# Slot-softmax denominators: from a ones product on TensorE and Ln/Exp on ScalarE to block transposes and a reduction on VectorE, in a fused attention and maxout-FFN kernel, with a new order of issue

## The chip, the cores and the metric

The kernel runs on one core of one Trainium2 chip. The metric is device time in microseconds (us), the median over several executions. The profile is of one execution; its "span" runs from the first to the last instruction that the profiler saw, and the measured time of the same execution is a little longer.

## The reference

Eight batches (b), eight heads (h), 576 positions (s), head size 64 (d), 32 memory slots (m). All inputs and outputs are float32.

```python
a = exp(phi - max_s(phi)); a = a / sum_s(a)              # softmax over positions
k_m = einsum('bhsm,bhsd->bhmd', a, k)                    # 32 slot keys per head
v_m = einsum('bhsm,bhsd->bhmd', a, v)                    # 32 slot values per head
p = exp(q @ k_m.T / 8 - max); p = p / sum_m(p)           # softmax over the 32 slots
x = (p @ v_m) as [4608 tokens, 512]
h = max(x @ w1, x @ w2, x @ w3)                          # maxout, 768 wide
out = h @ w_out                                          # [4608, 512]
```

The change concerns `sum_m(p)`, the denominator of the softmax over slots, and how batch 0 and the weights are brought in.

## The kernel before

Everything is computed in bfloat16 with float32 accumulation. Because `max(x@w1, x@w2, x@w3) = x@w3 + max(x@(w1-w3), x@(w2-w3), 0)`, the kernel multiplies with weight differences, and the part `x@w3` goes straight to the output through the product `w3 @ w_out`. And because `x = p @ v_m`, the slot values are multiplied into the weights first ("folded"), so that the FFN's first layer reads the 32 slot probabilities per head and not `x`.

The work of a batch is a set of small steps. Each is a letter, a number and `@batch` in one long string near the end of the kernel, and the program is issued in exactly that order: every engine receives its instructions in the order in which the steps stand there, and waits on semaphores where data or buffers are not ready. Nothing is reordered by a planner. An exclamation mark swaps the engine (ScalarE or VectorE) that empties a PSUM tile. The steps:

- `Y0 Y1 Y2 Y3` load w1, w2, w3 (L106, issued at L108) and w_out (L115). `L0 L1 L2 L3` load phi, k, v, q of a batch (phi at L90, k and v at L94, q at L102); `H` loads half of k or v for batch 0. All of these go through the POOL queue and convert to bfloat16 on the way, except phi, which stays float32; phi of batch 0 goes through SP (L88).
- `Zn` issues n warm-up matmuls (L132). `I` makes the identity matrix.
- `W0..W2` transpose w3 on TensorE (L157), emptied at L149; `O0..O3` compute w3 @ w_out (L165).
- `V` replaces w1 and w2 in place by w1 - w3 and w2 - w3 on VectorE (L186).
- `E` is exp(phi) on ScalarE (L203). `B` is k_m and v_m on TensorE (L216), `N` divides by the softmax denominators over positions (L232 to L246), `K` transposes the result into `kvt` (L261), emptied by ScalarE or VectorE.
- `Q` transposes half of a batch's q in 32x32 blocks on VectorE (L273).
- `S` makes the scores (L295) and their exponentials `e2` on ScalarE (L304), in two groups g = 0, 1 of four heads. `M` multiplies `e2` by a block matrix of ones, `blkones`, which leaves in each slot's row the sum over the 32 slots (L316). `R` turns the sum into its reciprocal on ScalarE by Ln and Exp(-x) (L329, L335). `X` multiplies on VectorE and gives `attn` (L340). `M`, `R` and `X` come once for each group.
- `D0..D2` (and `D4` for batch 0) fold the slot values into the weight differences, `D3` into w3 @ w_out (L361). Eight matmuls of 64x32 tiles stand side by side in each.
- `F0..F11` is the first FFN layer (L387), four matmuls each. An even one is emptied with Relu, mostly by ScalarE (L143); an odd one by VectorE, which takes the maximum with the even one (L400) into `hT`.
- `T0..T4` is the second layer: six matmuls with w_out (L418) and two or four with the folded w3 @ w_out (L427, L436), emptied into `ot` (L145 or L149) and stored through SP (L448).

All PSUM tiles come from one pool of four buffers of two banks each (tag `acc`), taken in turn in the order of issue; the `sm` tiles of step `M` are among them. k and v have one buffer for even and one for odd batches, q and phi two each.

Batch 0 before, up to the first step of the FFN:

```
H3@0 H2@0 H1@0 H0@0 L3@0 E@0 Z48@0 B@0 Y2@0 N@0 Y3@0 Q0@0 Q1@0 I@0 Z4@0 K@0! Z8@0 S@0
Z6@0 M1@0 R1@0 Y0@0 Y1@0 L0@1 M0@0 R0@0 W2@0 W1@0 W0@0 Z9@0 O0@0 X0@0 O1@0 X1@0 O2@0
O3@0 L1@1 V1@0 V0@0 D1@0 D0@0! L3@1 D3@0 V2@0 F8@0
```

Of the kernel before, what the change touches and what calls it, by code (L numbers as in the profile page):

```python
# [8 lines left out]
FP32 = mybir.dt.float32  # L9
# [6 lines left out]
def kernel(  # L16
# [12 lines left out]
    nc = tc.nc  # L29
# [145 lines left out]

    FIRST = {0: (0, 512), 1: (512, 768), 2: (768, 1024), 4: (1024, 1536)}

# [3 lines left out]
    def w_diff(n):  # L181

        c, end = FIRST[n]
        while c < end:
            e = min(end, (c // DF + 1) * DF)
            nc.vector.tensor_tensor(  # L186
                out=w12[:, :, c:e],
                in0=w12[:, :, c:e],
                in1=w_sb[:, :, 2, c % DF : c % DF + e - c],
                op=ALU.subtract,  # L190
            )
            c = e

# [58 lines left out]
    def att_kv_t(b, swap, part=None):  # L255

        s = st[b]
        ns = {None: slice(0, 3), 0: slice(1, 3), 1: slice(0, 1)}[part]
        ps = acc_pool.tile([P, 3, P], BF16, name="kvtp", tag="acc")
        for n in range(3)[ns]:  # L260
            nc.tensor.transpose(ps[:, n], s["kvn"][:, n], ident)  # L261
        if part != 1:
            s["kvt"] = work.tile([P, 3, P], BF16, name="kvt")
        evacuate("K", 0, swap, s["kvt"][:, ns], ps[:, ns])

    def att_q(b, n):
# [13 lines left out]
    def att_score(b):  # L280
# [3 lines left out]
        e2 = s["e2"] = work.tile([P, NG, S], BF16, name="e2")  # L284
        if b % 2 == 0:
            attns[b // 2] = work.tile([P, NG, 2 * S], BF16, name="attn")
# [23 lines left out]

    def att_sum(b, g):
        s = st[b]
# [11 lines left out]

    def att_rec(b, g):
        s = st[b]
# [10 lines left out]

    def att_mul(b, g):
        s = st[b]
        nc.vector.tensor_tensor(  # L340
            out=attns[b // 2][:, g, (b % 2) * S : (b % 2 + 1) * S],
            in0=s["e2"][:, g, 0:S],
            in1=s["r", g],
            op=ALU.mult,
        )

    wps, wp3s = {}, {}

    def fold(b, n, swap):
# [7 lines left out]
        ps = acc_pool.tile([P, NG, BANK], FP32, name="wps", tag="acc")  # L357
        for j in range(NP):
            for a in range(NG):
                r = slice(HP * a, HP * (a + 1))  # L360
                nc.tensor.matmul(  # L361
                    ps[M * j : M * (j + 1), a, 0 : hi - lo],
                    lhsT=s["kvt"][r, 0, M * j : M * (j + 1)],
                    rhs=(w3o if n == 3 else w12)[r, j, lo:hi],
                    start=True,
                    stop=True,
                    tile_position=(HP * a, M * j),
                )
        evacuate(
# [112 lines left out]
    def issue(b, n, swap):  # L482
# [12 lines left out]
            "S": lambda: att_score(b),  # L495
            "M": lambda: att_sum(b, i),
            "R": lambda: att_rec(b, i),
            "X": lambda: att_mul(b, i),
            "D": lambda: fold(b, i, swap),
# [9 lines left out]
    for w in """  # L509
        H3@0 H2@0 H1@0 H0@0 L3@0 E@0 Z48@0 B@0 Y2@0 N@0 Y3@0 Q0@0 Q1@0 I@0 Z4@0 K@0! Z8@0 S@0  # L510
        Z6@0 M1@0 R1@0 Y0@0 Y1@0 L0@1 M0@0 R0@0 W2@0 W1@0 W0@0 Z9@0 O0@0 X0@0 O1@0 X1@0 O2@0
        O3@0 L1@1 V1@0 V0@0 D1@0 D0@0! L3@1 D3@0 V2@0 F8@0 F10@0 F4@0 V4@0 F2@0 D2@0! F6@0!
        D4@0 F0@0 F3@0 F1@0 E@1 F5@0 F7@0 L2@1 F9@0 F11@0 B0@1 N0@1 T3@0 Q0@1 L1@2 L0@2 K0@1!
        T1@0 Q1@1 S@1 B1@1 N1@1 M0@1 L2@2 R0@1 K1@1 M1@1 X0@1 T0@0 R1@1 D1@1! L3@2 D0@1 D2@1
        E@2 X1@1 T2@0 F6@1! F10@1 F8@1 F7@1 F11@1 F0@1 F1@1 D3@1 B@2 F4@1 N@2 F9@1 L1@3 F5@1
        K@2! F2@1 Q1@2 F3@1 D3@2 L0@3 D2@2 T4@1! Q0@2 S@2 T0@1 M1@2 E@3 R1@2 M0@2 R0@2 T1@1!
        D0@2 L2@3 X1@2 D1@2! B@3 T2@1! L3@3 X0@2 L1@4 N@3 L0@4 F2@2 F6@2 Q1@3 Q0@3 F4@2 K@3
        F10@2 F0@2 F3@2 S@3 L2@4 F1@2 F8@2 L3@4 F11@2 M1@3 F7@2 R1@3 D3@3 E@4 D0@3! F9@2 T3@1
        F5@2 M0@3 R0@3 B@4 D2@3 D1@3! X1@3 N@4 L0@5 X0@3 T0@2! F0@3 F2@3 Q1@4 F4@3 Q0@4 L2@5
        F10@3 K@4 F6@3 F11@3 E@5 F3@3 D1@4! D0@4 T2@2! S@4 L1@5 F7@3 F8@3 F1@3 M0@4 F5@3 F9@3  # L520
        R0@4 X0@4 M1@4 R1@4 B@5 N@5 X1@4 D2@4 L3@5 D3@4 Q0@5 T2@3! K@5 F6@4 L3@6 F0@4 Q1@5 F4@4
        F7@4 S@5 F5@4 L0@7 F2@4 Q1@6 L0@6 Q0@6 F8@4 M1@5 R1@5 F1@4 E@7 F9@4 T1@2 F3@4 M0@5 R0@5
        L1@6 E@6 F10@4 T1@3 T3@3 X1@5 X0@5 F11@4 D3@5 D0@5 L2@6 B@6 D1@5! T0@3! N@6 L1@7 F2@5
        L2@7 F4@5 K@6 T4@3! S@6 B@7 D2@5 N@7 F3@5 F8@5 L3@7 F0@5 Q0@7 M0@6 R0@6 F1@5 T0@4! M1@6
        Q1@7 K@7 R1@6 T3@2 X0@6 X1@6 S@7 F5@5 F10@5 F6@5 F9@5 M1@7 R1@7 F7@5 X1@7 F11@5 M0@7
        R0@7 T3@4 X0@7 D2@7! D2@6 D0@7 T4@5! D1@6 D0@6 D1@7! T0@5! F0@7 F8@6 F4@6 F0@6 F6@6
        F9@6 F1@7 F10@6 F5@6 F11@6 F2@7 F6@7 F7@6 F2@6 F1@6 D3@6 D3@7 T1@4 F4@7 F3@6 F5@7 F3@7
        F8@7 F10@7 F11@7 F9@7 F7@7 T3@6 T1@5 T2@5! T2@7! T1@6 T0@7! T1@7 T2@6! T0@6! T2@4! T3@5
        T4@7! T3@7
    """.split():  # L530
# [32 lines left out]
```

## Time and profile before

| quantity | value |
|---|---|
| median of 8 runs | 171.08 us (170.21 to 171.70) |
| profiled execution: time | 171.5 us |
| profiled execution: span | 169.7 us |
| busy: TensorE matmuls / weight loads | 162.7 us / 91.3 us |
| busy: VectorE / ScalarE / GpSimd | 86.3 us / 112.6 us / 28.3 us |
| HBM read / written | 39.32 MB / 9.44 MB |
| first FFN matmul (F8@0) starts at | 30.38 us |

The profile gives, for each group of instructions, its line, engine, operation, operands (out<-in), shape, count, busy time in us, mean duration in ns, and how long the engine was idle before these instructions and what released it. PE is TensorE's matmul, PEld its weight load, DVE is VectorE, ACT ScalarE, POOL GpSimd, SP the sync engine. A busy engine is not yet the one that sets the time: the chain of waits, followed back from the last instruction, tells that. The profiled execution is 0.4 us above the median, and 1.8 us of its time lie around the span.

### The profile page before, as it was taken

The numbers are of one execution on the slowest core, as the hardware profiler recorded it, in microseconds if no ns is written. First come the engines' busy times: TensorE is split into PE (matmuls) and PEld (weight loads), VectorE is DVE, ScalarE is ACT, GpSimd is POOL, SyncE is SP. The second block draws the span as 40 slices with busy tenths as digits, with TensorE's granted clock in tenths as the row PEclk, the third lists the DMA queues.
The fourth block names the chain that finished last, engine by engine and source line by source line (L and its number), as shares of the span: only waits on it lengthen the run. The fifth ranks groups of instructions, "written<-read, shape, count | busy, mean of one in ns | idle before, by whom it ended". The sixth has DMA issues, their size and how long they took to land.

```text
span 169.7 us, 4672 instructions
## 1 busy us (share of the span) xinstructions
PE 162.7 (96%) x2015; PEld 91.3 (54%) x2035; DVE 86.3 (51%) x146; ACT 112.6 (66%) x170; POOL 28.3 (17%) x43
## 2 busy tenths in 40 slices
PE   7999999999799999999999999999999999999991
PEld 2344554574357446756566655564736757444450
DVE  6403174986368729588469773155862738100000
ACT  4100444863897898999999998797989682242420
POOL 7951111103302323100533100000000000000000
PEclk9999999999999999999999999999999999999999
DMA  5999999999999999999999999921113001243533
GB/s 155 174 204 210 203 211 265 222 207 261 259 227 307 233 217 325 258 278 229 239 237 349 234 208 234 256 98 62 62 68 124 0 4 62 85 162 128 184 124 126
DMA packets 21973, 31.77 MB, mean 187 GB/s; under 512 B 1216, under 2 KB 16576, under 8 KB 21952
## 3 DMA queue, kind: packets, MB, share of 16 engines
q0 software_dynamic: 16080, 21.43, 65.7%
q1 hardware_dynamic: 5728, 9.90, 16.5%
q8 instruction: 16, 0.26, 0.6%
q10 hardware_dynamic: 144, 0.13, 0.2%
q14 instruction: 5, 0.04, 0.1%
HBM read 39.32 MB, written 9.44 MB: 287 GB/s over the span
## 4 chain that ended last, share of the span: by engine, by line
PE 95%; issue 1%; DVE 1%; ACT 0%; ACTq 0%
PE acc L387 29%; PE po L418 27%; PE po L132 11%; PE po L427 8%; PE wps L361 5%; PE kvp L216 4%; PE po L165 3%; PE sm L316 2%; PE sc L295 2%; PE po L436 1%; PE kvtp L261 1%; PE po L459 1%; PE pt L157 1%; DVE kvn L236 0%; DVE kvn L246 0%
## 5 line engine op out<-in xcount | busy, mean ns | idle before, releaser
L387 PE MATMUL acc<-attn,wp 128*128 128x288 bf16 x384 | 52.2, 286 | 0.0
L418 PE MATMUL po<-wo_sb,hT 128*128 128x512 bf16 x194 | 50.3, 380 | 0.9
L400 DVE TENSOR_TENSOR hT<-acc,h 128x576 bf16<-128x576 f32 x48 | 34.8, 752 | 20.4 <-PE acc L387 19.2
L387 PEld LDWEIGHTS <-wp 128*128 128x128 bf16 x384 | 36.4, 98 | 13.1 <-issue 1.6
L145 ACT COPY ot<-po 128x512 f32<-128x512 f32 x31 | 18.2, 588 | 24.1 <-PE po L427 18.2
L418 PEld LDWEIGHTS <-hT 128*128 128x128 bf16 x210 | 19.5, 98 | 23.8 <-issue 3.5
L143 ACT ACTIVATE h<-acc 128x576 bf16<-128x576 f32 x46 | 27.5, 657 | 3.6 <-PE acc L387 3.6
L145 ACT CAST wp<-wps 128x1024 bf16<-128x1024 f32 x27 | 26.1, 1016 | 1.7 <-PE wps L361 1.7
L132 PE MATMUL po<-warm 128*128 128x512 bf16 x73 | 19.4, 423 | 1.4 <-DVE warm L120 1.2
L427 PE MATMUL po<-wp,attn 128*128 128x512 bf16 x61 | 18.2, 379 | 0.0
L132 PEld LDWEIGHTS <-warm 128*128 128x128 bf16 x75 | 7.7, 107 | 11.2 <-issue 3.8
L340 DVE TENSOR_TENSOR attn<-e,r 128x576 bf16<-128x576 bf16 x16 | 11.8, 753 | 2.7 <-PE po L427 1.4
L273 DVE STREAM_TRANSPOSE qT<-qq 128x576 f32<-128x576 f32 x16 | 11.7, 757 | 0.0
L329 ACT ACTIVATE ln<-sm 128x576 f32<-128x576 f32 x16 | 10.4, 647 | 1.5 <-PE sm L316 1.1
L335 ACT ACTIVATE r<-ln 128x576 f32<-128x576 f32 x16 | 10.9, 683 | 0.5
L304 ACT ACTIVATE e<-sc 128x576 bf16<-128x576 f32 x16 | 9.6, 662 | 2.2 <-PE sc L295 2.2
L476 DVE COPY ot<-po 128x256 f32<-128x256 f32 x1 | 0.4, 425 | 20.5 <-PE po L467 20.5
L203 ACT ACTIVATE e<-ph 128x1152 bf16<-128x1152 f32 (+1 forms) x9 | 9.5, 1060 | 1.6 <-DMA ph<-in_phi_dram 1.5
L94 POOL DMA_DIRECT2D kvo<-in_k_dram x9 | 6.7, 742 | 23.2 <-PE kvp L216 15.5
L427 PEld LDWEIGHTS <-attn 128*128 128x128 bf16 x62 | 6.1, 98 | 7.2
L102 POOL DMA_DIRECT2D qq<-in_q_dram x8 | 6.0, 748 | 22.2 <-DVE qT L273 18.0
L145 ACT COPY kvt<-kvtp 128x384 bf16<-128x384 bf16 (+1 forms) x3 | 1.3, 445 | 12.2 <-PE kvtp L261 12.2
(48 smaller groups left out, 118.4 us busy)
## 6 DMA issues: line engine op xcount, KB each, us to landing
out_dram<-ot SPq DMA_DIRECT2D x35, 256.0 KB, 2.4
qq<-in_q_dram POOLq DMA_DIRECT2D x8, 576.0 KB, 17.9
ph<-in_phi_dram POOLq DMA_DIRECT2D x7, 576.0 KB, 15.1
kvo<-in_k_dram POOLq DMA_DIRECT2D x7, 576.0 KB, 17.2
kvo<-in_v_dram POOLq DMA_DIRECT2D x7, 576.0 KB, 16.7
w_sb<-in_moe_w_dram POOLq DMA_DIRECT2D x3, 768.0 KB, 18.9
wo_sb<-in_moe_w_out_dram POOLq DMA_DIRECT2D x1, 768.0 KB, 16.5
ph<-in_phi_dram SPq DMA_DIRECT2D x2, 288.0 KB, 2.9
```

Of the source, the lines that this page charges most:

```text
L132: nc.tensor.matmul(po[:, 0:BANK], lhsT=warm[:, 0:P], rhs=warm, start=True, stop=True)
L143: nc.scalar.activation(out=out_, in_=in_, func=AF.Relu)
L145: nc.scalar.copy(out=out_, in_=in_)
L273: nc.vector.transpose(out=s["qT"][:, j].rearrange("p j c r e -> p (j c r e)").bitcast(FP32), in_=loaded[b]["q"][:, j].rearrange("p j c d - ...
L304: nc.scalar.activation(out=e2[:, a].rearrange("p (t r c) -> p t r c", t=2, c=NC), in_=sc[a][:, :, 0:SH].rearrange("p t (c r) -> p t r c", ...
L329: nc.scalar.activation(out=ln.rearrange("p (h n) -> p h n", h=2), in_=sm[:, :, 0:SH], func=AF.Ln,)
L335: nc.scalar.activation(out=r, in_=ln, func=AF.Exp, scale=-1.0)
L340: nc.vector.tensor_tensor(out=attns[b // 2][:, g, (b % 2) * S : (b % 2 + 1) * S], in0=s["e2"][:, g, 0:S], in1=s["r", g], op=ALU.mult,)
L387: nc.tensor.matmul(acc[:, h, 0:SH], lhsT=wps[b][:, g, w * DF + ft * P : w * DF + (ft + 1) * P], rhs=attn[:, g, c0 : c0 + SH], start=(g == ...
L400: nc.vector.tensor_tensor(out=hT[:, ft, (b % 2) * S : (b % 2 + 1) * S].rearrange("p (h n) -> p h n", h=2), in0=a, in1=s["h1", ft], op=ALU.max,
L418: nc.tensor.matmul(po, lhsT=hT[:, fc, c0 : c0 + P], rhs=wo_sb[:, fc, :], start=(n == 0), stop=False,)
L427: nc.tensor.matmul(po, lhsT=attn[:, g, c0 : c0 + P], rhs=wp3s[b][:, g, :], start=False, stop=(g == NG - 1),)
```

## The change

For batches 1 to 7 the steps `M` and `R` are replaced by steps on VectorE. `e2` is read as float32 words (two neighbouring bfloat16 positions each) and transposed in 32x32 blocks (`a`), so that the 32 slots of a head lie along the free dimension; they are summed there (`s`), the sums are inverted (`c`), the exponentials are multiplied by them (`m`), and the result is transposed back into `attn` (`X`). Batch 0 keeps the ones product, under new names. For batch 0 the folds into w1 and w2 no longer read weight differences: each is a sum of two products, one with w1 or w2 and the slot values, one with w3 and the negated slot values `kvtn`. The in-place subtraction `V` comes after the folds of batch 0, for batches 1 to 7. k and v of batch 0 are computed apart (`B0`, `B1`, and so on). The order is new throughout; at the start w3 and w_out are the first loads of the POOL queue, and the warm-ups become 29, then 9, 2 and 5.

```diff
-    FIRST = {0: (0, 512), 1: (512, 768), 2: (768, 1024), 4: (1024, 1536)}
+    FIRST = {0: (0, 384), 1: (384, 768), 2: (768, 1152), 4: (1152, 1536)}
...
-        c, end = FIRST[n]
+        c, end = n * BANK, (n + 1) * BANK
...
         evacuate("K", 0, swap, s["kvt"][:, ns], ps[:, ns])
+        if b == 0 and part != 0:
+            s["kvtn"] = const.tile([P, P], BF16, name="kvtn")
+            nc.scalar.mul(out=s["kvtn"], in_=ps[:, 0], mul=-1.0)
...
-    def att_sum(b, g):
+    def ones_sum(b, g):
...
-    def att_rec(b, g):
+    def ones_rec(b, g):
...
-    def att_mul(b, g):
+    def ones_mul(b, g):
...
+    def att_t(b, g):
+        s = st[b]
+        t = s["t", g] = work.tile([P, S // HP, R, 2], BF16, name="t", tag=f"t{g}")
+        nc.vector.transpose(
+            out=t.rearrange("p n r e -> p (n r e)").bitcast(FP32),
+            in_=s["e2"][:, g].bitcast(FP32),
+        )
+
+    def att_sum(b, g):
+        s = st[b]
+        sm = s["sm", g] = work.tile([P, S // HP, 2], FP32, name="sm", tag=f"sm{g}")
+        nc.vector.tensor_reduce(
+            out=sm,
+            in_=s["t", g].rearrange("p n r e -> p n e r"),
+            op=ALU.add,
+            axis=mybir.AxisListType.X,
+        )
+
+    def att_rec(b, g):
+        s = st[b]
+        nc.vector.reciprocal(out=s["sm", g], in_=s["sm", g])
+
+    def att_mul(b, g):
+        s = st[b]
+        t = s["t", g]
+        nc.vector.tensor_tensor(
+            out=t,
+            in0=t,
+            in1=s["sm", g].unsqueeze(2).to_broadcast([P, S // HP, R, 2]),
+            op=ALU.mult,
+        )
+
+    def att_back(b, g):
+        nc.vector.transpose(
+            out=attns[b // 2][:, g, (b % 2) * S : (b % 2 + 1) * S].bitcast(FP32),
+            in_=st[b]["t", g].rearrange("p n r e -> p (n r e)").bitcast(FP32),
+        )
...
-        for j in range(NP):
-            for a in range(NG):
-                r = slice(HP * a, HP * (a + 1))
-                nc.tensor.matmul(
-                    ps[M * j : M * (j + 1), a, 0 : hi - lo],
-                    lhsT=s["kvt"][r, 0, M * j : M * (j + 1)],
-                    rhs=(w3o if n == 3 else w12)[r, j, lo:hi],
-                    start=True,
-                    stop=True,
-                    tile_position=(HP * a, M * j),
-                )
+        terms = [(s["kvt"][:, 0], w3o[:, :, lo:hi] if n == 3 else w12[:, :, lo:hi])]
+        if b == 0 and n != 3:
+            terms.append((s["kvtn"], w_sb[:, :, 2, lo % DF : lo % DF + hi - lo]))
+        for i, (lhs, rhs) in enumerate(terms):
+            for j in range(NP):
+                for a in range(NG):
+                    r = slice(HP * a, HP * (a + 1))
+                    nc.tensor.matmul(
+                        ps[M * j : M * (j + 1), a, 0 : hi - lo],
+                        lhsT=lhs[r, M * j : M * (j + 1)],
+                        rhs=rhs[r, j, :],
+                        start=(i == 0),
+                        stop=(i == len(terms) - 1),
+                        tile_position=(HP * a, M * j),
+                    )
...
-            "M": lambda: att_sum(b, i),
-            "R": lambda: att_rec(b, i),
-            "X": lambda: att_mul(b, i),
+            "a": lambda: att_t(b, i),
+            "s": lambda: att_sum(b, i),
+            "c": lambda: att_rec(b, i),
+            "m": lambda: att_mul(b, i),
+            "X": lambda: (ones_mul if b == 0 else att_back)(b, i),
+            "M": lambda: ones_sum(b, i),
+            "R": lambda: ones_rec(b, i),
```

The new order up to the scores of batch 2:

```
Y2@0 I@0 Z29@0 W1@0 W0@0 Y3@0 W2@0 H2@0 H0@0 Z9@0 O3@0! E@0 L3@0 O0@0 B0@0 N0@0 O2@0
K0@0! Q0@0 H3@0 H1@0 O1@0 Q1@0 Y0@0 S@0 Z2@0 M0@0 R0@0 B1@0 Y1@0 N1@0 M1@0 R1@0 L0@1
K1@0 L1@1 D3@0 X0@0 Z5@0 D1@0! X1@0 D0@0 F10@0 F8@0 F0@0 F4@0 V0@0 F2@0! D2@0 D4@0 V1@0
F6@0 F1@0 F5@0 F11@0 F7@0 L3@1 F3@0 F9@0 E@1 B0@1 L2@1 N0@1 L0@2 Q0@1 T2@0! Q1@1 K0@1!
T1@0 S@1 V2@0 B1@1 L1@2 E@2 a0@1 s0@1 a1@1 N1@1 s1@1 T3@0 K1@1 c1@1 D0@1 D1@1! c0@1
m0@1 L2@2 D2@1 L3@2 m1@1 X0@1 T0@0! X1@1 F10@1 F4@1 L0@3 F11@1 F8@1 F0@1 F5@1 F2@1 F1@1
F9@1 F6@1 F7@1 F3@1 B@2 D3@1 T3@1 N@2 Q1@2 Q0@2 K@2 E@3 T4@1! L1@3 L2@3 S@2
```

## The prediction

> **What bounds the kernel now.** I read the chain of waits first, then the busy times, then the timeline of the first 31 us.
>
> ```profile
> PE 95%; issue 1%; DVE 1%; ACT 0%; ACTq 0%
> PE acc L387 29%; PE po L418 27%; PE po L132 11%; PE po L427 8%; PE wps L361 5%; PE kvp L216 4%; PE po L165 3%; PE sm L316 2%; PE sc L295 2%; PE po L436 1%; PE kvtp L261 1%; PE po L459 1%; PE pt L157 1%; DVE kvn L236 0%; DVE kvn L246 0%
> ```
>
> TensorE's own work is 95% of the chain; 11% of it are warm-ups (L132), which do nothing but pass time while data come. So there are two stages. From the first FFN matmul on, a table of engine busy times for that stretch alone gives:
>
> ```profile
> 30.38:166.08 135.70, 133.89 (x1761) 78.04 (x1777) 73.45 (x124) 103.00 (x155) 15.65 (x21) 1.00 0.79 185
> ```
>
> (window, sum; then busy us of PE, PEld, DVE, ACT, POOL.) TensorE is idle 1.8 of 135.7 us: here only less TensorE work, or an earlier start, shortens the kernel. Before 30.38 us the timeline shows what the first FFN matmul waited for:
>
> ```profile
> 23.98 5.34 PE L165 MATMUL po<-wo_sb,w3T 128*128 128x512 bf16 x23
> 26.05 1.83 DVE L186 TENSOR_TENSOR w_sb<-w_sb 128x1024 bf16<-128x1024 bf16 x2 [1.36 <-DMA w_sb<-in_moe_w_dram]
> 29.25 0.52 PE L361 MATMUL wps<-w_sb,kvt 64*32 64x256 bf16 x16
> 30.38 2.29 PE L387 MATMUL acc<-attn,wp 128*128 128x288 bf16 x16
> ```
>
> w1 landed at 26.0 us, but the folds L361 began at 29.25, because TensorE was busy until then with w3 @ w_out (L165), which could not begin before w_out had landed (issue at 5.67 us plus 16.5 to landing: 22.2), and whose first product also stood behind nine warm-ups.
>
> **The rows that the change touches.**
>
> ```profile
> L340 DVE TENSOR_TENSOR attn<-e,r 128x576 bf16<-128x576 bf16 x16 | 11.8, 753 | 2.7 <-PE po L427 1.4
> L273 DVE STREAM_TRANSPOSE qT<-qq 128x576 f32<-128x576 f32 x16 | 11.7, 757 | 0.0
> L329 ACT ACTIVATE ln<-sm 128x576 f32<-128x576 f32 x16 | 10.4, 647 | 1.5 <-PE sm L316 1.1
> L335 ACT ACTIVATE r<-ln 128x576 f32<-128x576 f32 x16 | 10.9, 683 | 0.5
> ```
>
> **What the Trainium skill says.** "VectorE: DVE Perf Modes", section on the TRN2 errata, gives (N+151)/0.96 GHz for an fp32 two-input operation: 757 ns at N = 576, and the two DVE rows above show 753 and 757. I use it as an estimate for the half-width transposes: (288+151)/0.96 = 457 ns. The same page's perf-mode tier table says `tensor_reduce` has only the 1x mode; at 576 elements that makes 757 ns by the same formula, an estimate, since no reduction is in this trace. "TensorE: Matmul & The Clock Gate", section "Wait — 56ns, not 53.3ns?", gives N/2.4 GHz + 2.5 ns from one warm matmul to the next, 122.5 ns at N = 288; the trace agrees, four `sm` matmuls take 0.49 us in the chain (61.21 us). The same page's Part 1 says that the clock starts at half rate until some 3.4 us of work; here warm-ups came 0.43 us apart until 6.67 us and 0.21 after.
>
> **The sum, part by part.**
>
> 1. *Ones products gone.* Seven batches x two groups x two matmuls = 28 matmuls x 0.1225 = **-3.4 us** on TensorE, all on the path. Batch 0 keeps its four. Their 14 PSUM tiles go too.
>
> 2. *Start.* The POOL loads before the FFN are the same bytes in another order. In the before trace the queue is steady: halves of k and v land 1.4 us apart (8.5, 9.9, 11.3), q 2.8 later (14.1), each weight 3.8 to 4.4 later (17.8, 22.2, 26.0, 29.9). So in the new order w3 lands at about 9.5, w_out 13.7, k 16.5, q 19.3, v 22.2, and w1 and w2 at 26.0 and 29.9 as before. The warm-ups Z29 end near 13x0.43+16x0.215 after 1.2 us, 10.2; W, Z9 and two of the O steps fill to 16.6; B0 is there when k is; O2, O1 fill up to q. Q0 and Q1 (2 x 0.757 after 19.3) give S@0 at 20.8 to 21.3. Then ScalarE is the chain: two exponentials (0.66 each), two Ln/Exp pairs (1.33 each), `kvtn` (0.3, estimated from the 0.38 of a 256-wide copy), D3's evacuation (1.02), D1's (768 elements between rows of 657 ns at 576 and 1016 at 1024: 0.80): 21.4 + 6.1 = 27.5. The other requirement, w1 at 26.0 + D1's matmuls 0.4 + 0.8, comes to 27.2. So F10@0 starts near 27.6, **-2.8 us**. The O steps (5.2 us) and the subtraction (1.8 us) leave the path because w_out comes 8 us earlier and the folds no longer need differences.
>
> 3. *Double folds of batch 0.* D1 and D0 lie in part 2. D2 and D4 become 32 matmuls of 384 columns instead of 16. By the 24 of 512 columns that take 0.77 us in the chain, that is 0.77 us against about 0.57: **+0.2 us**.
>
> 4. *VectorE chain.* Per group 0.457 + 0.757 + 0.18 (row of 167 ns for two columns, now 18) + 0.753 + 0.457 = 2.60 us instead of 0.753. `V` now stands among batch 0's FFN steps: V0 (1.22, row of 1219 ns) and V1 (two pieces of 0.69, row of 686 ns) are queued ahead of F2's Relu and of all `hT`, which T2@0 waits for; before, V2 and V4 stood there with 1.83 us, so I take nothing for the difference of 0.8, inside the bounds below. Splitting batch 0's B costs 72 more small matmuls (0.74 us in the chain) while TensorE waits for loads: nothing. Fourteen groups add 26 us to VectorE; ScalarE loses 14 x 1.33 = 18.6 us. I walked through both orders and gave every step its row's duration. Between S@1 and S@6 that sums, before, to 65.9 TensorE, 45.2 VectorE, 68.6 ScalarE, and after to 66.9, 64.1, 58.4 (the cut points fall on slightly different sets of steps). ScalarE, with sums above TensorE's, did not stall TensorE before, since the order lets engines run ahead; VectorE's new sum is below that. A local excess is left: from `m0@4` to `X0@6` 28.5 us of VectorE against 23.3 of TensorE. Also, after S@1 TensorE has filler (B1, T3, D0, D1, D2, T0: 5.3 us) against exponential plus chain of 0.7 + 5.2 and a `V2` of 1.2 in front. I charge **+0.6 us**, bounds 0 to 3.
>
> 5. *Loads.* In the new order k of batch 1 follows w2 and phi: 34.1 us as before, when TensorE now wants it at about 34.5 (before: 37.3). q and v land at 37.0 and 39.8, S@1 and B1@1 want them at 38.5 and 39.5. The cover is thin, at most 0.5 us, taken inside part 4's bounds. From batch 3 on POOL waits for buffers (22.1 us on PE kvp, 18.0 on DVE qT), so loads have slack. SP's stores move with their T steps.
>
> Sum: -3.4 - 2.8 + 0.2 + 0.6 = **-5.4 us** against the profiled 171.5; against the median, 0.4 lower, **165.7 us**.
>
> **Rivals.**
>
> *No gain at the start.* If the loads do not keep this pace, or k, q, v of batch 0, now behind w3 and w_out, arrive late, the first FFN matmul stays at 30.4. For it: batch 0's attention hangs on loads that come 5 us (q) to 12 us (v) later than before. Against: the steady landings. Then -3.4 + 0.2 + 0.6, so 168.5 us.
>
> *VectorE becomes the bound: slower.* Place: S@1 to S@6, ten groups. VectorE passes TensorE's 66.9 us when a group costs 0.28 us more than 2.60; from there each 0.1 costs 1 us, and the gain of 6 us is gone at about 3.5 us per group. If the reduction, which reads every second bfloat16, and the product with a broadcast operand both run at half the rate (+0.60 each, 3.8 per group), VectorE needs 76.1 us, 9.2 over: 174.3 us. For it: neither form is in this trace. Against: the odd-form reads in the trace (L246, every second column) show no such factor (342 ns for 128 elements).
>
> *A larger gain.* If ScalarE's 18.6 us less and 14 PSUM tiles fewer also take away most of the 1.8 us of TensorE idling, and the chain adds nothing: 163.6 us.
>
> **Chances.** Forecast as summed 0.68; no gain at the start 0.15; larger gain 0.10; VectorE bound 0.07. The forecast's own range is 164.3 to 167.3; with the larger gain and the missing start it is 163.2 to 169.4, which leaves out VectorE's case and little more. A measurement here can tell about 0.5% (0.9 us) from no change: faster by more than that 0.89, within it 0.04, slower 0.07.
>
> **What would show it.** Right: L387 starts at 27 to 28 us; `sm` matmuls only for batch 0; VectorE near 110 us busy, ScalarE near 95; reduction and product each near 0.75 us; TensorE idle under 3 us after its first FFN matmul. Wrong: TensorE waiting on VectorE's `attn` or `hT` between batches 1 and 6 for more than 3 us, warm-up-like gaps before 27 us, or L216 of batch 1 waiting for k.

## The result, and the profile after

The changed kernel takes 167.09 us in the median (11 runs, 165.46 to 167.92), the kernel before 171.08 us (32 runs, 170.21 to 171.70). The ratio is 0.9758, with a 95% interval of 0.9733 to 0.9783: 4.0 us faster, where 5.4 were forecast. Its runs spread over 2.5 us, those of before over 1.5. The profiled execution took 167.67 us with a span of 165.9. The experiments stand beside three further sets of runs of the kernel before, with medians of 170.83, 170.99 and 171.01. Ratios, and the differences between kernels, leave out runs that are over 1.5% above a kernel's fastest, while a median given beside them is of all runs.

From the page of the changed kernel, its busy times, and then the chain of waits with its shares by engine:

```profile
PE 153.7 (93%) x2063; PEld 85.9 (52%) x2081; DVE 104.8 (63%) x196; ACT 100.8 (61%) x150; POOL 28.3 (17%) x43
...
PE 71%; DMA 21%; issue 3%; POOL 2%; ACT 1%; POOLq 0%; ACTq 0%
```

Before, the chain was 95% TensorE and held no load at all. Now 21% of it are loads. The chain in order of time shows where:

```profile
4.18 13.52 DMA kvo<-in_k_dram
...
20.81 21.07 DMA kvo<-in_v_dram
41.92 0.75 PE kvp L213 x72
```

It runs through a load of k of batch 0, POOL's own issuing after that, and v of batch 1, which lands at 41.9 us, and only from there on through TensorE. The wait that takes it there is short (0.23 us before the matmuls L213 at 41.92), but a chain that is followed backwards turns off at any wait; so I read it as saying no more than that the work up to 42 us now keeps pace with the loads. The other load that TensorE waits for is w1. The timeline of the start (start us, duration us, engine, line, operands, and in brackets the idle time before with its releaser):

```profile
14.95 2.75 PE L165 MATMUL po<-wo_sb,w3T 128*128 128x512 bf16 x12 [0.70 <-DMA wo_sb<-in_moe_w_out_dram]
...
28.20 0.36 PE L403 MATMUL wps<-w_sb,kvt 64*32 64x384 bf16 x8 [0.43 <-DMA w_sb<-in_moe_w_dram]
...
28.79 1.50 ACT L145 CAST wp<-wps 128x768 bf16<-128x768 f32 x2 [0.77 <-PE wps L403]
...
29.65 2.62 PE L429 MATMUL acc<-attn,wp 128*128 128x288 bf16 x20 [0.60 <-ACT wp L145]
```

w3 @ w_out (L165) indeed moved from 24 us to 15, out of the way. But the first double fold (L403) starts at 28.20, the moment the last part of w1 has landed, and the first FFN matmul (L429, the former L387) at 29.65: 0.73 us earlier than before, not 2.8.

The stretch from the first FFN matmul on (window, sum; busy us of PE, PEld, DVE, ACT, POOL; granted clock, DMA share, GB/s):

```profile
29.65:162.30 132.65, 130.50 (x1750) 75.32 (x1765) 92.76 (x175) 90.07 (x134) 15.63 (x21) 1.00 0.82 193
```

132.65 us instead of 135.70. TensorE is idle 2.15 us of it (the window less its busy time), so it still sets the time here, although VectorE's busy time rose from 73 to 93 us. The new rows, grouped by line and shape (count | busy us, mean ns | idle before):

```profile
L350 DVE STREAM_TRANSPOSE t<-e 128x288 f32<-128x288 f32 x14 | 6.4, 463 | 7.0 <-ACT e L304 6.9
...
L358 DVE TENSOR_REDUCE sm<-t 128x18 f32<-128x576 bf16 x14 | 10.3, 738 | 0.3
L367 DVE RECIPROCAL sm<-sm 128x18 f32<-128x18 f32 x14 | 3.5, 257 | 0.2
L372 DVE TENSOR_TENSOR t<-t,sm 128x576 bf16<-128x576 bf16 x14 | 10.4, 746 | 0.2
L380 DVE STREAM_TRANSPOSE attn<-t 128x288 f32<-128x288 f32 x14 | 6.2, 461 | 0.2
L316 PE MATMUL sm<-e,blkones 128*128 128x288 bf16 x4 | 0.8, 287 | 0.2 <-ACT e L304 0.2
```

A group costs 463 + 738 + 257 + 746 + 461 = 2665 ns on VectorE, and the ones product is there only for batch 0.

### The profile page after: what moved, and what is told of

Same layout as the page of the kernel before. It is cut to its first block, busy times and chain, and to the rows that moved or that the text cites. A ratio compares the mean times of both kernels' runs of the same rounds, so it can differ in the third digit from the quotient of the medians.

```text
span 165.9 us, 4795 instructions
## 1 busy us (share of the span) xinstructions
PE 153.7 (93%) x2063; PEld 85.9 (52%) x2081; DVE 104.8 (63%) x196; ACT 100.8 (61%) x150; POOL 28.3 (17%) x43
## 4 chain that ended last, share of the span: by engine, by line
PE 71%; DMA 21%; issue 3%; POOL 2%; ACT 1%; POOLq 0%; ACTq 0%
PE po L460 26%; PE acc L429 25%; DMA kvo<-in_v_dram 13%; DMA kvo<-in_k_dram 8%; PE po L469 7%; PE wps L403 4%; PE kvp L213 3%; PE sc L295 2%; PE po L478 1%; PE po L501 1%; PE kvtp L258 1%; POOL w_sb L108 1%; POOL wo_sb L115 0%; POOL qq L102 0%; POOL kvo L94 0%
## 5 line engine op out<-in xcount | busy, mean ns | idle before, releaser
L429 PE MATMUL acc<-attn,wp 128*128 128x288 bf16 x384 | 50.1, 286 | 0.7 <-ACT wp L145 0.6
L429 PEld LDWEIGHTS <-wp 128*128 128x128 bf16 x384 | 36.7, 98 | 12.9 <-ACT wp L145 1.6
L145 ACT COPY ot<-po 128x512 f32<-128x512 f32 x34 | 20.0, 589 | 26.9 <-PE po L469 18.6
L145 ACT CAST wp<-wps 128x1024 bf16<-128x1024 f32 (+1 forms) x31 | 29.1, 990 | 6.0 <-PE wps L403 6.0
L460 PEld LDWEIGHTS <-hT 128*128 128x128 bf16 x210 | 19.2, 98 | 24.4 <-issue 4.4
L132 PE MATMUL po<-warm 128*128 128x512 bf16 x43 | 11.9, 425 | 1.3 <-DVE warm L120 1.2
L304 ACT ACTIVATE e<-sc 128x576 bf16<-128x576 f32 x16 | 9.6, 652 | 2.6 <-PE sc L295 2.6
L94 POOL DMA_DIRECT2D kvo<-in_v_dram x9 | 6.6, 743 | 26.3 <-PE wps L403 16.6
L350 DVE STREAM_TRANSPOSE t<-e 128x288 f32<-128x288 f32 x14 | 6.4, 463 | 7.0 <-ACT e L304 6.9
L358 DVE TENSOR_REDUCE sm<-t 128x18 f32<-128x576 bf16 x14 | 10.3, 738 | 0.3
L372 DVE TENSOR_TENSOR t<-t,sm 128x576 bf16<-128x576 bf16 x14 | 10.4, 746 | 0.2
L213 PE MATMUL kvp<-kvo,e 64*32 64x192 bf16 (+2 forms) x720 | 8.7, 229 | 1.1 <-DMA kvo<-in_v_dram 1.0
L403 PE MATMUL wps<-w_sb,kvt 64*32 64x512 bf16 (+1 forms) x200 | 8.6, 372 | 1.0 <-ACT ot L145 0.6
```

The costliest lines, as they stand in the source:

```text
L132: nc.tensor.matmul(po[:, 0:BANK], lhsT=warm[:, 0:P], rhs=warm, start=True, stop=True)
L145: nc.scalar.copy(out=out_, in_=in_)
L213: nc.tensor.matmul(kvp[M * j : M * (j + 1), a, 0:nd], lhsT=s["e"][r, j, c, :], rhs=kv[r, cols, j, c, :], start=(c == 0), stop=(c == NC - 1 ...
L358: nc.vector.tensor_reduce(out=sm, in_=s["t", g].rearrange("p n r e -> p n e r"), op=ALU.add, axis=mybir.AxisListType.X,)
L372: nc.vector.tensor_tensor(out=t, in0=t, in1=s["sm", g].unsqueeze(2).to_broadcast([P, S // HP, R, 2]), op=ALU.mult,)
L403: nc.tensor.matmul(ps[M * j : M * (j + 1), a, 0 : hi - lo], lhsT=lhs[r, M * j : M * (j + 1)], rhs=rhs[r, j, :], start=(i == 0), stop=(i == ...
```

## The experiments

Three questions: is the gain after the first FFN matmul what the sum said (TensorE's ones products gone, VectorE's chain hidden)? Which parts of the change carry it? And why is the start worth so little?

**The changed kernel once more (c_after).** No edit.

> The changed kernel again, unchanged, to stand beside the others of this call. Main theory: the time after the first FFN matmul is set by TensorE, and the start gave only 0.7 us because w1 lands at 28.2 and not at 26.0 us. So the median is 167.1 within 0.7 us, the first FFN matmul (L429) at 29 to 30.5 us, and the last of w1's sixteen parts lands over 1.5 us after the middle one. Rival: that late landing was an accident of one profiled execution; then w1 lands near 26 and the first FFN matmul starts near 27.6 us.

Measured: 167.43 us (4 runs, 165.57 to 168.19), ratio 0.9769 [0.9696, 0.9841]. The median is that of the first expectation, but the profiled execution took only 165.57 us (span 163.8), and in it the rival came true. Its timeline at the start, and its stretch from the first FFN matmul on:

```profile
26.21 0.35 PE L403 MATMUL wps<-w_sb,kvt 64*32 64x384 bf16 x8 [0.43 <-DMA w_sb<-in_moe_w_dram]
...
27.65 2.62 PE L429 MATMUL acc<-attn,wp 128*128 128x288 bf16 x20 [0.60 <-ACT wp L145]
```

```profile
27.65:160.20 132.55, 130.41 (x1750) 75.32 (x1765) 92.72 (x175) 89.89 (x134) 15.61 (x21) 1.00 0.83 196
```

The first FFN matmul stands at 27.65, where 27.6 was worked out. The time is 165.57 us; the sum, which started from the profiled 171.5, gives 166.1 for a profiled execution, and 165.7 is its figure for the median. From the first FFN matmul on it runs like the other one, 132.55 against 132.65 us; nearly all of the difference of 2.1 us lies ahead of it. And it is the loads. The same DMA, w1, issued in both in the window from 7.0 to 7.8 us (tile, queue, count, KB, us from issue to landing), first in the profile of the result, then in this one:

```profile
w_sb<-in_moe_w_dram POOLq DMA_DIRECT2D x1, 768.0 KB, 21.1
```

```profile
w_sb<-in_moe_w_dram POOLq DMA_DIRECT2D x1, 768.0 KB, 19.1
```

In the traces each load raises its semaphore 16 times, once for each of the parts in which it is moved. I read these moments for several runs (us; "mid" is the median part, "last" the one that releases the waiting engine):

| run | start | w3 mid / last | w1 mid / last | first FFN matmul | profiled us |
|---|---|---|---|---|---|
| before | old | 17.2 / 17.9 | 24.9 / 25.9 | 30.38 | 171.5 |
| after | new | 9.1 / 10.8 | 25.5 / 28.2 | 29.65 | 167.67 |
| c_after | new | 8.0 / 8.7 | 24.8 / 26.2 | 27.65 | 165.57 |
| e1_ones_all | new | 8.1 / 9.4 | 25.2 / 25.9 | 27.41 | 177.63 |
| e6_reduce_twice | new | 8.0 / 8.7 | 24.7 / 25.9 | 27.42 | 171.51 |
| e7_no_sum | new | 8.1 / 10.3 | 25.1 / 27.4 | 28.84 | 168.27 |
| e10_idle_ones | new | 8.9 / 11.0 | 25.5 / 27.6 | 29.09 | 172.39 |
| e5_w3_halves | new, w3 halved | 8.7 / 10.5 | 25.2 / 26.9 | 28.38 | 166.48 |
| e2_start_back | old | 17.0 / 18.0 | 24.8 / 25.6 | 29.04 | 170.01 |

What follows: in every row with the new start the first FFN matmul comes 1.5 us after w1's last part, early or late; that landing sets it. The part lags 0.8 to 2.7 us behind the middle one, from one execution to the next. Wherever w1 is over 2 us behind, w3, the queue's first load, already was 1.7 us or more behind, so most of such a lag arises at the start and is carried along. Not all of it does: in the profile of the result it grows from 1.7 to 2.7 us on the way, in c_after from 0.6 to 1.4. In the kernel before w1's last part was there at 25.9 and the first fold came at 29.25. Of these 3.3 us the subtractions that the folds need took 1.83 (26.05 to 27.88), so by this sum a landing up to about 1.4 us later would have changed nothing. That covers the lags of 0.8 to 1.5 us that the four executions with the old start show, but not one of 2.7.

**The ones product back in all batches, under the new order (e1_ones_all).** Batches 1 to 7 use `M`, `R` and the product again, at the places of `a`, `s` and `X`:

```diff
-            "X": lambda: (ones_mul if b == 0 else att_back)(b, i),
+            "X": lambda: ones_mul(b, i),
...
-  S@1 V2@0 B1@1 L1@2 E@2 a0@1 s0@1 a1@1 N1@1 s1@1 T3@0 K1@1 c1@1 D0@1 D1@1! c0@1 m0@1
+  S@1 V2@0 B1@1 L1@2 E@2 M0@1 R0@1 M1@1 N1@1 R1@1 T3@0 K1@1 D0@1 D1@1!
```

> Order and start of the changed kernel, but the ones product, Ln/Exp and one product on VectorE in all batches. Main theory (28 matmuls less are 3.4 us of TensorE, and the VectorE chain costs nothing): 167.1 + 3.4 = 170.5 us, plus 0 to 2.4 us because ScalarE's sum between S@1 and S@6 (58.4 + 10 x 1.33 = 71.7 us) would exceed TensorE's (69.3). Rival (the VectorE chain stalls TensorE for as long as the ones products took): 167 to 168 us.

Measured: 177.63 us (177.30 to 179.08), ratio 1.0418 [1.0364, 1.0473]: 10.5 us slower than the changed kernel (167.1), not 3.4 to 5.8. Its stretch from the first FFN matmul on, and then what TensorE waited for (us in total, times, longest):

```profile
27.41:172.30 144.89, 136.52 (x1778) 78.56 (x1793) 69.49 (x119) 106.26 (x162) 15.62 (x21) 1.00 0.77 180
```

```profile
PE sm L316 <- ACT e L304: 1.6, 2, 0.8
PE po L460 <- ACT wp L145: 1.2, 3, 0.8
...
PE po L460 <- ACT ln L329: 0.8, 1, 0.8
```

TensorE idles 8.4 us instead of 2.15, in pieces, and most of the waits are for ScalarE. Between 40 and 50 us ScalarE is busy 9.57 of 10 us and TensorE 8.36. The new order gives ScalarE more to do in between, on the footing that Ln and Exp are gone; at the places where I put them back they don't fit. Other places weren't tried.

**Only the matmuls back (e10_idle_ones).** VectorE's sums stay; the 28 products with `blkones` are issued in addition, and nobody reads them.

```diff
-  S@1 V2@0 B1@1 L1@2 E@2 a0@1 s0@1 a1@1 N1@1 s1@1 T3@0
+  S@1 V2@0 B1@1 L1@2 E@2 M0@1 a0@1 s0@1 M1@1 a1@1 N1@1 s1@1 T3@0
```

> The changed kernel with the 28 ones products of batches 1 to 7 issued besides, into PSUM tiles that nobody reads; no Ln, no Exp. They cost TensorE 28 x 0.1225 = 3.4 us and take 14 turns of the PSUM buffers. Theory (TensorE's own time counts one for one): 167.3 + 3.4 = 170.7 us, and the rest of the 10 us by which the kernel with the ones product in all batches was slower is ScalarE's Ln and Exp. Rival (the matmuls or the PSUM turns make most of the 10 us): 173 us or more.

Measured: 172.08 us (20 runs), ratio 1.0058 [1.0035, 1.0080], 5.0 us above 167.1, between the theory (170.7) and the rival (173). Its stretch:

```profile
29.09:167.00 137.91, 134.38 (x1778) 78.07 (x1793) 93.33 (x175) 90.36 (x134) 15.67 (x21) 1.00 0.79 188
```

5.3 us longer than the changed kernel's: TensorE is busy 3.9 us more and idle 1.4 more, which agrees with its wait of 1.6 us for the exponentials (L316 on L304) at two products that stand directly behind them. So the matmuls account for 3.4 to 3.9 us, about as the sum had it, and about 1.4 go to waits that depend on where the products stand. Of e1's 10.5 us this leaves 5.5. That Ln and Exp on ScalarE take them is argued, from this subtraction and from the busy times of e1; no run puts back Ln and Exp alone.

**VectorE's sums in the old order with the old start (e3_start_old_dve_sum).** The file's order is that of before, with `a s c m X` put where `M R X` were; single folds and differences as before.

```diff
-  Q1@1 S@1 B1@1 N1@1 M0@1 L2@2 R0@1 K1@1 M1@1 X0@1 T0@0 R1@1 D1@1! L3@2
+  Q1@1 S@1 B1@1 N1@1 a0@1 s0@1 L2@2 c0@1 K1@1 a1@1 s1@1 m0@1 X0@1 T0@0 c1@1 D1@1! L3@2
```

> Start and order of the kernel before throughout; alone the sums over slots of batches 1 to 7 go to VectorE, at the places where the ones product, the reciprocal and the product stood. Main theory (only TensorE's 3.4 us count, the order lets VectorE run ahead): 171.1 - 3.4 = 167.7 us. Rival (without the new order the longer chain on VectorE, 5.2 us a batch against 1.5, is waited for by the FFN's first layer): 169 to 172 us.

Measured: 183.73 us (6 runs), ratio 1.0726 [1.0678, 1.0774]: 12.5 us slower than before (183.3 against 170.8), and slower than either expectation. The profiled execution took 185.87 us, longer than most, so only the kind of its waits is read, what TensorE waited for:

```profile
PE acc L429 <- DVE attn L380: 3.5, 3, 2.5
PE kvtp L258 <- DVE kvn L233: 1.8, 2, 1.4
PE wps L403 <- DVE wp L149: 1.5, 1, 1.5
PE acc L429 <- DVE rden L229: 1.5, 1, 1.5
```

and the chain of waits by engine:

```profile
PE 68%; DVE 27%; issue 2%; ACT 0%; DVEq 0%; ACTq 0%
```

The end is that of the prediction's rival "VectorE becomes the bound", by another way. VectorE is not full (60% busy); as I read the waits, the old order asks for `attn` too soon after `S`, and the long chain stands in the order of issue ahead of the small steps on VectorE that TensorE waits for (`kvn`, `wp`, `rden`).

**The old order without any sum (e11_old_order_no_sum).** The kernel before, `M` and `R` of batches 1 to 7 replaced by a constant 1/32, so no denominator is computed there.

```diff
     def att_sum(b, g):
+        if b > 0:
+            return
...
     def att_rec(b, g):
+        if b > 0:
+            s["r", g] = consts
+            return
```

> The kernel before, in its order, without ones product, Ln and Exp in batches 1 to 7 (the product on VectorE takes a constant 1/32 in place of the reciprocals): what the old order would gain if the denominators cost nothing on any engine. Theory A (the old order has no fault of its own, and the 16 us between it and the old order with the VectorE sums are VectorE's chain alone): 171.0 - 3.4 = 167.6 us. Theory B (the old order itself stalls once the ones products no longer fill TensorE): 169 us or more.

Measured: 169.09 us (4 runs), ratio 0.9871 [0.9841, 0.9901]: 2.0 us gained, as theory B had it, where TensorE has 3.4 us less to do. So part of it did not come through in the old order. The one wait of size in its profile is 2.2 us for a load of v, at 108 us, but that execution took 171.82 us, 2.8 above the middle one of the others, and cannot carry the point; where the other 1.4 us stay is left open. It places e3: the sums on VectorE cost 183.3 - 169.0 = 14.3 us in the old order.

**The sums left out of the new order (e7_no_sum).** In batches 1 to 7 the reduction and the reciprocal are left out and the product takes a constant 1/32; both transposes and the product stay.

```diff
-        sm = s["sm", g] = work.tile([P, S // HP, 2], FP32, name="sm", tag=f"sm{g}")
-        nc.vector.tensor_reduce(
...
+        s["sm", g] = consts
...
-        nc.vector.reciprocal(out=s["sm", g], in_=s["sm", g])
+        pass
```

> The changed kernel without the reductions and reciprocals of batches 1 to 7 (the product takes a constant 1/32 instead of the sums): 14 x (0.74 + 0.26) = 14 us less on VectorE. If the chain is hidden in the changed kernel, the time stays at 167.3 within 0.5 us. If the chain still stalls TensorE, it is faster by what it costs, at most the 3 us that the prediction kept as the bound: 164.3 us.

Measured: 168.37 us (4 runs), ratio 0.9829 [0.9781, 0.9877], some 1.3 us above the changed kernel rather than below it. One microsecond less of VectorE work per group, 14 us in all, gains nothing: in the new order the reductions and reciprocals are hidden. The first FFN matmul came at 28.84, and from there TensorE waits for a load, v of batch 1; the profile of the result has 0.2 us there:

```profile
PE kvp L215 <- DMA kvo<-in_v_dram: 1.9, 1, 1.9
```

**The reduction twice (e6_reduce_twice).** The other direction: each group reduces once more into a tile that nobody reads, 0.74 us per group.

```diff
+        extra = work.tile([P, S // HP, 2], FP32, name="extra", tag=f"extra{g}")
+        nc.vector.tensor_reduce(
+            out=extra,
+            in_=s["t", g].rearrange("p n r e -> p n e r"),
+            op=ALU.add,
+            axis=mybir.AxisListType.X,
+        )
```

> The changed kernel with each of the 14 reductions on VectorE done twice, the first into a tile that nobody reads: 14 x 0.74 = 10.3 us more on VectorE, nothing else. By the prediction's rule (VectorE passes TensorE between S@1 and S@6 from 0.28 us a group on, ten groups, then one for one): (0.74 - 0.28) x 10 = 4.6 us, so 167.3 + 4.6 = 172 us. Theory of a wide cover (the order hides VectorE altogether): 167.3 us. Theory that no cover is left (every microsecond of the chain is waited for): 177 us.

Measured: 172.48 us (15 runs), ratio 1.0081 [1.0058, 1.0104], 5.4 us above the changed kernel, where the rule of the prediction (free up to 0.28 us per group, then ten groups count in full) gives 10 x (0.74 - 0.28) = 4.6. A group already takes 2.67 us and not the 2.60 of the sum; with the 0.07 taken off the slack the rule gives 5.3. TensorE's waits are now for VectorE:

```profile
PE wps L410 <- DVE kvt L149: 1.2, 1, 1.2
PE acc L436 <- DVE kvn L243: 0.9, 1, 0.9
PE acc L436 <- DVE attn L387: 0.9, 1, 0.9
PE po L467 <- DVE hT L449: 0.7, 1, 0.7
```

So less VectorE work gains nothing and 0.74 us more per group costs 5.4 us: the chain fits into its cover with little to spare. How little isn't measured, as this is one point of the rule only.

**The old start in front of the new order (e2_start_back).** Loads, warm-ups, differences and single folds as before up to the first FFN steps; from `F10@0` on the new order with VectorE's sums.

```diff
-  Y2@0 I@0 Z29@0 W1@0 W0@0 Y3@0 W2@0 H2@0 H0@0 Z9@0 O3@0! E@0 L3@0 O0@0 B0@0 N0@0 O2@0
+  H3@0 H2@0 H1@0 H0@0 L3@0 E@0 Z48@0 B@0 Y2@0 N@0 Y3@0 Q0@0 Q1@0 I@0 Z4@0 K@0! Z8@0 S@0
...
-  D1@0! X1@0 D0@0 F10@0 F8@0 F0@0 F4@0 V0@0 F2@0! D2@0 D4@0 V1@0 F6@0
+  V1@0 V0@0 D1@0 D0@0! L3@1 D3@0 V2@0 F10@0 F8@0 F0@0 F4@0 F2@0! D2@0 V4@0 D4@0 F6@0
```

> The start of the kernel before (its order up to the first FFN step, 48 warm-ups, weight differences and single folds in batch 0), then the order and the VectorE sums of the changed kernel. Main theory (the new start is worth the 0.7 us that the trace shows, less 0.2 for double folds): 167.6 us, first FFN matmul near 30.4. Rival (the new start is worth the 2.8 us of the prediction and the loss is elsewhere): 169.7 us.

Measured: 170.04 us (14 runs), ratio 0.9956 [0.9933, 0.9980]. The new start with its double folds is worth 2.9 us, near the rival's figure. But in its profile not by an earlier first FFN matmul: that comes here at 29.04, earlier than in the profile of the result. The largest wait of TensorE after it is for a difference, on which the second pair of folds depends:

```profile
PE wps L403 <- DVE w_sb L186: 1.7, 1, 1.7
```

Some of the loss is the clock. It stands at 0.50 from 34.6 to 38.1 us, and TensorE is busy 131.6 us from the first FFN matmul on, where the changed kernel has 130.5.

This run also shows what set the old start. The same 48 warm-ups, in the kernel before and then here:

```profile
1.19 13.20 PE L132 MATMUL po<-warm 128*128 128x512 bf16 x48 [1.19 <-DVE warm L120]
```

```profile
1.19 11.86 PE L132 MATMUL po<-warm 128*128 128x512 bf16 x48 [1.19 <-DVE warm L120]
```

They take 1.34 us less, and the first FFN matmul comes 1.34 us earlier. In all four executions with the old start it follows the end of these warm-ups by 16.0 us (30.38, 29.04, and 30.09 and 30.10 in e3 and e11), and in the kernel before TensorE has no idle time over 0.25 us from the first warm-up to 42 us. So the old start was paced by TensorE's own order of issue, warm-ups included, and not by the landing of w1. Whether fewer warm-ups in the old order would have brought part of the gain was not tried.

**Single folds and differences under the new start (e8_subtract_back).** Batch 0 folds differences again; `V1`, `V0` stand ahead of `D1`, `D0`, and `V2`, `V4` ahead of `D2`, `D4`.

```diff
-  K1@0 L1@1 D3@0 X0@0 Z5@0 D1@0! X1@0 D0@0 F10@0 F8@0 F0@0 F4@0 V0@0 F2@0! D2@0 D4@0 V1@0
+  K1@0 L1@1 D3@0 X0@0 Z5@0 V1@0 D1@0! X1@0 V0@0 D0@0 F10@0 F8@0 F0@0 F4@0 F2@0! V2@0 D2@0 V4@0 D4@0
```

> The changed kernel with the weight differences back in batch 0: each fold waits for a subtraction on VectorE (384 columns x 4, between the 0.69 us row of 1024 elements and the 1.22 us row of 2048: 0.95 us) and is then single. Theory (the folds wait for w1 and w2 as soon as they land, so the subtraction comes on top): first FFN matmul 0.8 us later, the folds into w2 1 to 1.9 us later, TensorE 0.6 us less; median 168.0 to 169.0 us. Rival (ScalarE's chain of exponentials covers it): 167.0 us.

Measured: 171.74 us (20 runs), ratio 0.9997 [0.9974, 1.0019]: 3.9 us above the changed kernel (171.0 against 167.1), all of its gain, and more than any of the expectations. What TensorE waited for, and then the timeline around the second pair:

```profile
PE wps L403 <- DVE w_sb L186: 4.7, 4, 1.7
```

```profile
30.08 3.82 PE L429 MATMUL acc<-attn,wp 128*128 128x288 bf16 x20
...
33.93 0.76 DVE L147 TENSOR_SCALAR h<-acc 128x576 bf16<-128x576 f32 x1 [4.37 <-PE acc L429]
34.61 1.82 DVE L186 TENSOR_TENSOR w_sb<-w_sb 128x1536 bf16<-128x1536 bf16 x2
...
35.61 0.36 PE L403 MATMUL wps<-w_sb,kvt 64*32 64x384 bf16 x8 [1.72 <-DVE w_sb L186]
```

Each of the four folds waits for its own difference. The second pair is worse, since I had put `V2` behind the Relu of `F2`: the difference stands behind an instruction that waits for an FFN product (33.93), and the fold starts at 35.61, 5.5 us after the first FFN matmul, where the double fold of the changed kernel starts 2.6 us after it (32.20). And the clock is part of it: it stands at 0.50 from 29.15 to 32.56 us, and the first 20 FFN matmuls take 3.82 us, where they take 2.62 in both profiles of the changed kernel. So some of the 3.9 us are of my placing and some of the clock; how much a better place would give back wasn't tried.

**Three tries at the late w1.** The first halves w1 and w2 by columns, so that `D1` and the first FFN steps need only the first half (e9_w12_halves):

```diff
+        lo, hi = slice(0, DF // 2), slice(DF // 2, DF)
+        for f in ([hi, lo], [lo, hi], [slice(0, DF)])[i]:
             nc.gpsimd.dma_start(
-                out=w_sb[:, :, i], in_=w.rearrange("(j p) f -> p j f", p=P)
+                out=w_sb[:, :, i, f],
+                in_=w.rearrange("(j p) f -> p j f", p=P)[:, :, f],
             )
```

> The changed kernel with w1 and w2 of two DMAs each, by halves of their columns, the half that the first fold of each needs first. Theory (the spread of the changed kernel's times comes from the last parts of w1 and w2, which land between 26 and 28 us and between 30 and 32, with no other work left to cover them): the needed half is there 1.9 us earlier, the exponential chain on ScalarE sets the first FFN matmul near 27.6 us also where parts land late; median 166.0 to 166.6 us and a narrower spread than 165.5 to 168.2. Rival (the late parts don't matter, or smaller pieces land no earlier): 167.3 us with the same spread.

Measured: 168.12 us (4 runs), ratio 0.9809 [0.9752, 0.9865], no gain. In its profile the half that was needed first had landed at 26.4, 1.9 us before the other (28.3), and still the first FFN matmul came at 29.16: v of batch 0 was late as well (24.4), and with it ScalarE's work for batch 0. The lag sits on the queue, not on w1 alone.

The second loads half of k ahead of w3, as the first DMA of the queue (e4_k_half_first); the third loads w3 in two halves (e5_w3_halves):

```diff
-  Y2@0 I@0 Z29@0 W1@0 W0@0 Y3@0 W2@0 H2@0 H0@0 Z9@0
+  H2@0 Y2@0 I@0 Z29@0 W1@0 W0@0 Y3@0 W2@0 H0@0 Z9@0
```

> The changed kernel with one half of k of batch 0 (288 KB) loaded ahead of w3, as the first DMA of the POOL queue; nothing else moved. Theory (the late parts of all landings come from the first DMA of the queue, and a small first one leaves them less behind, as in the kernel before, where w1's last part came 0.8 to 1.5 us after the middle one): the lag of w1's last part is near 1 us, median 166.0 us. Rival (the lag is drawn anew in each execution, whatever stands first): 167.3 us, lag between 0.7 and 2.7 us.

```diff
+        for h in halves if i == 2 else [slice(0, NP)]:
             nc.gpsimd.dma_start(
-                out=w_sb[:, :, i], in_=w.rearrange("(j p) f -> p j f", p=P)
+                out=w_sb[:, h, i], in_=w.rearrange("(j p) f -> p j f", p=P)[:, h]
             )
```

> The changed kernel with w3 loaded as two DMAs of two row blocks each. Same question from the other side: the first DMA is half as large, the bytes and their order stay. Theory of the small first DMA: lag of w1's last part near 1 us and a median near 166.2 us. Rival: 167.3 us, lag between 0.7 and 2.7 us.

Measured: 166.83 us (6 runs), ratio 0.9744 [0.9715, 0.9772], and 166.54 us (6 runs), ratio 0.9740 [0.9705, 0.9776]. Both are a little below the changed kernel's 0.9758, well within the intervals: no gain is shown. In e4 the small first load (last part 7.8 us) was itself 2.1 us behind its middle part; w1's last part came at 26.8, 1.3 behind its middle one, and the first FFN matmul at 28.57, here 1.8 us later: TensorE's folds didn't wait for w1, and ScalarE had no pause ahead of it. So the lag does not need a large first load. What causes it stays open.

## Why the prediction was right, and where it was off

The direction and the mechanism held; of 5.4 us, 4.0 came. By the steps of the sum:

1. *Ones products gone, -3.4.* Held. Putting the 28 matmuls back unread costs 5.0 us (e10), of which about 1.4 are waits of their place. The stretch from the first FFN matmul on shrank by 135.70 - 132.65 = 3.05 us, where steps 1, 3 and 4 came to -3.4 + 0.2 + 0.6 = -2.6.
2. *Start, -2.8.* **This is the term that was mis-sized**: about -0.9 in the median (the 4.0 less the 3.1 of the later stretch), -0.7 in the profile of the result, -2.7 in that of c_after. The step that failed is "w1 and w2 at 26.0 and 29.9 as before". The middle part of w1 did keep its place (24.7 to 25.5 us in the table, 24.9 before), but the last one landed anywhere from 25.9 to 28.2. I took the landing of one profiled execution for a constant, because in the kernel before TensorE's own order set the start and the landing could not be seen to matter. The change takes that cover away, and the first FFN matmul then follows w1 by 1.5 us. The working noted the cover ("TensorE was busy until then") and did not ask what the landing would be worth without it. With 26.2, as in c_after, the step comes out at 27.65 against 27.6, but partly by luck. The sum had ScalarE as the later of two requirements (27.5) and w1 as the earlier (27.2). In c_after ScalarE was done with D3's evacuation at 26.02, which by my estimate would have let the FFN begin at 26.9 (the 0.85 us from the start of the next evacuation, 26.80, to 27.65 added), and w1 was the later one. The 30.38 from which the step counted was itself the latest of four executions with the old start (29.04 to 30.38).
3. *Double folds, +0.2.* Harmless as priced, but undervalued: I let only the subtraction ahead of the first fold leave the path. With differences under the new start the time goes back to the kernel before's (e8, +3.9), as all four folds, the second pair too, wait for VectorE; how much of that is my placing of the second pair, and how much the lower clock, is open.
4. *VectorE chain, +0.6.* The durations were right (2.67 us per group against 2.60; the reciprocal 257 ns where 180 was assumed from a row of two columns). The estimates made from the Trainium skill's "VectorE: DVE Perf Modes", sections on the TRN2 errata and the perf-mode tier table, agree with the rows to 3%: 457 ns for the half-width transposes (463 and 461), and the 1x mode of `tensor_reduce` (757 estimated, 738 measured). The charge of 0.6 was not needed (e7, and TensorE idles 2.15 us, much as before). e6 agrees with the slack of 0.28 us per group and the rule for what comes after it, at one point.
5. *Loads.* Batch 1's k did not stall; v landed at 40.0 in c_after (39.8 worked out, wanted at 39.5) and TensorE waited 0.29 us there. In the profile of the result both w1 and v are 2 us later, and so an earlier first FFN matmul alone would have met v next; in e7, where it came 0.8 us earlier, TensorE waits 1.9 us for v.

On the rivals: "no gain at the start" (168.5) is what the longest executions of the changed kernel come near to (167.92), for the first reason given there: the loads did not keep the pace. It is w1 that was waited for, but v of batch 0 was late too in the profile of the result (24.4, where 22.2 was worked out), and ScalarE alone would have held the FFN until about 28.9 there (estimated as above, from D3's evacuation, which ended at 28.02). "VectorE becomes the bound" is true of the old order (e3) and, with 0.74 us more per group, of the new one (e6); not of the change as it is. "A larger gain" did not occur. The list of signs: `sm` only for batch 0, the reduction and product near 0.75 us, and the idle time of TensorE held; the start of the first FFN matmul at 27 to 28 us held in c_after and not in the profile of the result (29.65). VectorE is busy 104.8 us (near 110 said), ScalarE 100.8 (near 95 said): the new order gave some 5 us of evacuations from VectorE to ScalarE (copies into `ot`: VectorE 4 before and 1 after, ScalarE 31 and 34), which the subtraction of removed instructions did not count.

One assumption lies under all steps and was wrong in general, though it did no harm to the sum: that the parts add. Sums on VectorE in the old order: +12.5 us. Ones product in the new order: +10.5. Differences in the new start: +3.9. Each is far more than the price of its instructions on TensorE's path. As they were tried here, neither the new sums nor the new order is a gain without the other. The new start in front of the old order was not tried.

## What to carry to other kernels

When a change removes the work that lay over a transfer, the landing of the *last* part of that transfer, in the worst of several executions, becomes the start of what follows; one profile shows one draw. Price an operation with its place in the issue order: in the new order taking two of the five VectorE instructions away gains nothing, in the old one the five cost 14.3 us, so a hand-written order and the operations in it have to be changed and measured together. Walking both orders with durations from rows, engine by engine, gave 4.6 us for the doubled reduction, where 5.4 were measured, and is worth its trouble. And when TensorE issues warm-ups from the first microsecond on, look whether they are what sets the start: here two executions of the same start lay 1.34 us apart through them alone.

## What the runs showed of the hardware

- The 16 parts of one load do not land together, and the lag of the last behind the middle is not constant: 0.8 to 2.7 us for the same 768 KB of w1 in nine executions with the new start, 0.8 to 1.5 in four with the old one. It appears with the first load of the queue (0.6 to 2.3 us for w3 as the first load) and stays over the next seven, where some is added (from 1.7 to 2.7 us in the profile of the result, from 0.6 to 1.4 in c_after) or lost (from 1.3 to 0.8 in e1). In the profile of the result one part lost about 1 us between 20 and 23 us, at the time of a 16 KB packet of the instruction queue (21.4 us). That this is the cause was not tested; e5 has such a packet at 21.3 us, and its lag stays at 1.65 us.
- The first warm-ups, issued from 1.19 us on, come 0.43 us apart and then 0.22; the moment of the change differs from one execution to the next, from 4.0 us (e2) to 6.7 us (before, c_after) in fourteen traces. That is after 2.8 to 5.5 us of work, so the 3.4 us of work that the prediction quotes is no fixed length here.
- A reciprocal of 18 float32 columns takes 257 ns, one of 2 columns 167: 5.6 ns for each further column, much more than a transpose (461 ns at 288 columns against 753 at 576, 1.0 ns each).
- The reduction over every second bfloat16 (738 ns for 576) and the product with an operand broadcast along 32 (746 ns) cost no more than the dense product (753 ns).
- The clock granted to TensorE can drop to 0.50 for 3.4 us in the middle of the kernel: in e8 from 29.15 to 32.56 us, in the second of two idle times of 1.3 and 1.2 us, in e2 from 34.6 to 38.1, 0.8 us after one of 1.7. Not every such idle time brings a drop: in e7 TensorE idles 1.9 us at 41 us, and in e1 it is busy only 8.36 us between 40 and 50, and both keep 1.00, as the changed kernel does over the whole stretch.
